# Splitting the output matmuls of a chunked mLSTM into two column halves of the TensorE array

## Chip, core and metric

The kernel runs on one core of a Trainium2 chip. The metric is the device time of one execution in microseconds; before the change the median of 3 runs is 906.31 us (905.92 to 907.33). Lower is better.

## What is computed

Three stages follow each other: an mLSTM recurrence over 768 tokens (4 batches, 8 heads, 40 values a head), then two gated feed-forward layers over the 3072 tokens.

```
for t in range(S):                                   # S = 768, per batch and head
    m_new  = max(f[t] + m, i[t])
    f_stab = exp(f[t] + m - m_new);  i_stab = exp(i[t] - m_new);  m = m_new
    C = f_stab * C + i_stab * outer(v[t], k[t])      # 40 x 40
    n = f_stab * n + i_stab * k[t]
    y[t] = sigmoid(o[t]) * (C @ q[t]) / max(|n @ q[t]|, 1)
x = y as [3072, 320]
x = (sigmoid(x @ w_gate) * (x @ w_val)) @ w_out      # 320 -> 1536 -> 320
h = x @ w_in                                         # 320 -> 2048 -> 320
out = (h * clip(h + 3, 0, 6) / 6) @ w_out2
```

## The kernel before

The recurrence is worked in 6 chunks of 128 tokens (`NC`, `L`), for 4 batches each, so there are 24 (chunk, batch) blocks. A chunk's tokens see each other through a 128 x 128 matrix per head, and the earlier chunks through a state `cst`. A block has three pieces:

- `att0`: eight matmuls for the products of keys and queries (line 303; 40 rows, alternately in the row halves from partition 0 and 64), then the decay matrix `dec` by scans and products on VectorE (lines 320 and 333), and the values with a gate factor, `vi`.
- `att1`, which the change touches: from chunk 1 on, four matmuls give what the state adds to the output (line 346, weights = 128 tokens of queries, streamed = a head pair's state, 82 columns, into `o_ps`); eight matmuls give what the chunk's own tokens add (line 356, weights = 128 columns of `dec`, streamed = `vi`, 41 columns, into `i_ps`). VectorE or ScalarE then reads both banks into `y` (lines 369, 372 and 374), divides (lines 376 to 381) and multiplies with the output gate into `yo` (line 383).
- `att2`: three transposes of `yo` (line 398), eight matmuls for the new state (line 405, 40 columns of weights, output alternately on partitions 0 and 64 of one bank), and the split of the transposed output into a rounded part and a rest (lines 415 and 416).

All these matmuls are in fp32. The feed-forward layers run in fp32r with each operand as a rounded part plus a rest: lines 439 to 446 for the way up, 480 and 490 for the way down of the first layer, 635 to 637 for that of the second. Their weights come packed as integers; `to_f32` unpacks them on VectorE (lines 108, 112 and 116, output `bits`), and half of them go back to memory first (line 515).

TensorE works in program order. Between the pieces of the blocks stand steps of the first layer: in the loop over `steps` each step takes one piece of a block, then one `m1_h` (16 matmuls) and one `m1_out` (8 matmuls). The tile scheduler may move rows, and does so in the first two chunks; from the third on a block's line 346 and line 356 stand together, with 24 large matmuls before and after. The second layer begins after the last block. The attention tiles `qk`, `vko` and `dec` have two buffers each; loads wait on SyncE's queue until a buffer is free, in one order with the weight loads and stores (lines 88, 91, 189, 190, 193, 515).

Of the kernel before, what the change touches and what calls it, by code (L numbers as in the profile page):

```python
# [18 lines left out]
B, H, S, D = 4, 8, 768, 40  # L19
# [3 lines left out]
NP = H // 2  # L23
D1 = D + 1
# [8 lines left out]
def mlstm_then_two_gated_ffn(  # L33
# [11 lines left out]
    nc = tc.nc  # L45
# [32 lines left out]
    cst = const.tile([P, B, NP, 2 * D1], F32, name="cst")  # L78
# [155 lines left out]
    def later_chunks():  # L234
# [40 lines left out]
        out=sel, in_=ident[:BH, :BH].rearrange("p (n two) -> p n two", two=2),  # L275
# [4 lines left out]
        out=odd[:, :, 0], in_=ident[:BH, :BH].rearrange("p (n two) -> p two n", two=2),  # L280
# [4 lines left out]
        out=par.rearrange("p (two n) -> p two n", two=2), in_=odd.to_broadcast([BH, 2, 64])  # L285
    )

    def scale_heads(out, in_, by, apart):

        if apart:  # L290
            for h in range(H):
                nc.scalar.mul(out=out[:, h, :], in_=in_[:, h, :], mul=by[:, h, :])
        else:
            nc.vector.tensor_tensor(out=out, in0=in_, in1=by.to_broadcast(list(out.shape)), op=ALU.mult)
# [45 lines left out]
    def att1(c, b, ps):  # L340
        a = at[c, b]
        dec, vi = a["dec"], a["vi"]
        if c > 0:
            o_ps = ps()
            for n in range(NP):
                nc.tensor.matmul(  # L346
                    out=o_ps[:, n * 2 * D1 : (n + 1) * 2 * D1],
                    lhsT=a["qk"][:, 0, n, :],
                    rhs=cst[:, b, n, :],
                    start=n == 0,  # L350
                    stop=n == NP - 1,
                    skip_group_check=True,
                )
        i_ps = ps()
        for h in range(H):
            nc.tensor.matmul(  # L356
                out=i_ps[:, h * D1 : (h + 1) * D1],
                lhsT=dec[:, h, :],
                rhs=vi[:, h, :],
                start=h == 0,  # L360
                stop=h == H - 1,
                skip_group_check=True,
            )
        i_v = i_ps[:, : H * D1].rearrange("p (h d) -> p h d", d=D1)
        y = ap.tile([P, H, D1], F32, tag="y", name="y")
        den = ap.tile([P, H, 1], F32, tag="den", name="den")
        if c > 0:
            o_v = o_ps[:, : H * D1].rearrange("p (h d) -> p h d", d=D1)
            nc.vector.tensor_tensor(
                out=y, in0=o_v, in1=gT[:, c, b].to_broadcast([P, H, D1]), op=ALU.mult  # L370
            )
            nc.vector.tensor_tensor(out=y, in0=y, in1=i_v, op=ALU.add)
        else:
            nc.scalar.copy(out=y, in_=i_v)
        nq = y[:, :, D:D1]
        nc.vector.scalar_tensor_tensor(
            out=den, in0=nq, scalar=-1.0, in1=nq, op0=ALU.mult, op1=ALU.max
        )
        nc.vector.tensor_scalar(out=den, in0=den, scalar1=1.0, scalar2=None, op0=ALU.max)
        nc.vector.reciprocal(out=den, in_=den)  # L380
        scale_heads(y[:, :, 0:D], y[:, :, 0:D], den, c == 1 or c == 0 and b < 2)
        yo = ap.tile([P, 3 * P], F32, tag="yo", name="yo")
        nc.vector.tensor_tensor(
            out=yo[:, :DM].rearrange("p (h d) -> p h d", d=D),
            in0=y[:, :, 0:D],
            in1=a["vko"][:, 2, :].rearrange("p (h d) -> p h d", d=D),
            op=ALU.mult,
        )

        nc.scalar.copy(out=yo[:, DM:], in_=yo[:, 2 * P : DM])  # L390
        a["yo"] = yo
# [162 lines left out]
    for b in range(2):  # L554
        work(1 + b, n_w1)
        for att in (att0, att1, att2):
            att(0, b, any_ps)
# [5 lines left out]
    halves = 4  # L563
# [11 lines left out]
    for i, (c, f, ts) in enumerate(steps):  # L575
# [4 lines left out]
        for _ in range(2 if i < 2 else 1):  # L580
            if pieces:
                cp, b, piece = pieces.pop(0)
                if cp > 0 and b == 0 and piece == 0:
                    x_tiles((1, cp))
                (att0, att1, att2)[piece](cp, b, ps_att)
                nxt = divmod(cp * B + b + 2, B)
                if cp > 0 and piece == 2 and nxt[0] < NC:
                    att_load(*nxt)
                    dec_load(*nxt)
# [141 lines left out]
```

## Time and profile before

| | us |
|---|---|
| median of 3 runs | 906.31 |
| the profiled execution, its own time | 904.88 |
| its span, first to last instruction | 903.0 |
| TensorE matmul busy | 873.6 (97%), 5077 instructions |
| TensorE weight loads busy | 752.1 (83%) |
| VectorE busy | 535.0 (59%) |
| ScalarE busy | 362.2 (40%) |
| 16 DMA engines, queue q1, mean share | 27.4% |

Busy time adds up what an engine spent in instructions; matmuls overlap each other, so the distance between the starts of two matmuls tells their pace, and the busy time of one does not. In the views, PE is TensorE, PEld its weight loads, DVE VectorE, ACT ScalarE, SP SyncE. A row of the timeline gives the start, the busy time of a merged run, the line, the output and its inputs, the shapes and the count. Column pairs such as 128*64 are active rows and columns of the array. TensorE's granted clock reads 1.00 in all stages.

### The profile page before, as it was taken

What the parts mean: (1) busy time and instruction counts of PE and PEld (TensorE: products, weight loads), DVE (VectorE), ACT (ScalarE), POOL (GpSimd) and SP (SyncE); (2) the same over time, 40 slices, a digit from 0 to 9 for tenths busy, and PEclk for the clock granted to TensorE, in tenths of its full rate; (3) what the DMA queues carried; (4) which work ended last, traced back from release to release, by engine and by line L of the source; (5) the groups of instructions that cost most, each with busy time, mean ns of one, the idle gap of its engine ahead of it and who ended that gap; (6) DMA issues with size and microseconds to landing.
All of it is one profiled execution on the core that took longest, in us unless ns stands there. A gap on an engine that the chain in (4) does not pass through costs nothing.

```text
span 903.0 us, 12844 instructions
## 1 busy us (share of the span) xinstructions
PE 873.6 (97%) x5077; PEld 752.1 (83%) x5077; DVE 535.0 (59%) x947; ACT 362.2 (40%) x720; POOL 2.5 (0%) x8
## 2 busy tenths in 40 slices
PE   2799999999999999999999999999999999999998
PEld 2688878887788888888888888999999999999997
DVE  7889999988765655555444555435344353443433
ACT  5675664333322232223223545334343343343432
POOL 1000000000000000000000000000000000000000
PEclk9999999999999999999999999999999999999999
DMA  9535545877422222223300431101001010000000
GB/s 327 226 133 183 201 162 168 290 258 250 156 75 70 84 90 69 69 91 104 104 1 1 131 98 67 36 1 65 1 30 36 1 65 1 3 28 1 30 1 30
DMA packets 25195, 84.22 MB, mean 93 GB/s; under 512 B 2608, under 2 KB 5872, under 8 KB 25136
## 3 DMA queue, kind: packets, MB, share of 16 engines
q1 hardware_dynamic: 25088, 83.31, 27.4%
q8 instruction: 40, 0.66, 0.3%
q14 instruction: 19, 0.16, 0.1%
q10 hardware_dynamic: 48, 0.10, 0.0%
HBM read 69.40 MB, written 13.99 MB: 92 GB/s over the span
## 4 chain that ended last, share of the span: by engine, by line
PE 90%; DVE 5%; DMA 2%; ACT 1%; issue 1%; SPq 0%; DVEq 0%; ACTq 0%
PE mm L443 12%; PE mm L445 12%; PE mm L444 12%; PE acc L480 10%; PE mm L439 7%; PE mm L446 6%; PE acc L637 5%; PE acc L636 5%; PE acc L635 5%; PE att L356 4%; PE acc L490 3%; PE att L303 2%; PE att L346 2%; PE att L637 2%; PE att L636 2%; PE att L635 2%
## 5 line engine op out<-in xcount | busy, mean ns | idle before, releaser
L443 PE MATMUL mm<-xh,w 128*128 128x512 f32 (+1 forms) x496 | 191.8, 387 | 0.0
L445 PE MATMUL mm<-xh,w 128*128 128x512 f32 (+1 forms) x496 | 191.0, 385 | 0.0
L444 PE MATMUL mm<-xl,w 128*128 128x512 f32 (+1 forms) x496 | 190.7, 385 | 0.0
L453 DVE TENSOR_TENSOR gl<-g,gh 128x512 fp32r<-128x512 f32 (+1 forms) x172 | 116.3, 676 | 99.3 <-ACT gh L452 98.8
L452 ACT CAST gh<-g 128x512 fp32r<-128x512 f32 (+1 forms) x172 | 104.9, 610 | 158.0 <-PE att L636 90.3
L617 DVE SCALAR_TENSOR_TENSOR g<-g,mm 128x512 f32<-128x512 f32 x96 | 66.0, 688 | 112.0 <-ACT g L616 112.0
L616 ACT ACTIVATE g<-mm,half 128x512 f32<-128x512 f32 x96 | 66.2, 690 | 112.1 <-PE mm L446 112.0
L445 PEld LDWEIGHTS mm<-xh,w 128*128 128x128 f32 x496 | 93.6, 189 | 19.2
L444 PEld LDWEIGHTS mm<-xl,w 128*128 128x128 f32 x496 | 93.8, 189 | 19.1
L443 PEld LDWEIGHTS mm<-xh,w 128*128 128x128 f32 x496 | 93.9, 189 | 15.0
L480 PE MATMUL acc<-gh,w 128*128 128x512 f32 (+1 forms) x304 | 102.5, 380 | 0.9 <-ACT w L150 0.5
L439 PE MATMUL mm<-xl,w 128*128 128x512 f32 (+1 forms) x248 | 101.0, 407 | 0.4 <-ACT g L465 0.4
L466 DVE TENSOR_TENSOR g<-g,mm 128x512 f32<-128x512 f32 (+1 forms) x76 | 50.0, 658 | 76.9 <-PE mm L446 75.7
L446 PE MATMUL mm<-xh,w 128*128 128x512 f32 (+1 forms) x248 | 95.3, 384 | 0.0
L465 ACT ACTIVATE g<-mm 128x512 f32<-128x512 f32 (+1 forms) x76 | 43.6, 574 | 116.6 <-PE mm L446 115.2
L637 PE MATMUL acc<-w,gl 128*128 128x320 f32 x288 | 89.0, 309 | 0.0
L636 PE MATMUL acc<-w,gh 128*128 128x320 f32 x288 | 88.9, 309 | 0.0
L635 PE MATMUL acc<-w,gh 128*128 128x320 f32 x288 | 88.8, 308 | 0.0
L480 PEld LDWEIGHTS acc<-gh,w 128*128 128x128 f32 x304 | 56.5, 188 | 13.0 <-ACT gh L452 1.6
L480 PE MATMUL acc<-gl,w 128*128 128x512 f32 (+1 forms) x152 | 57.8, 381 | 0.6 <-DVE gl L453 0.6
L635 PEld LDWEIGHTS acc<-w,gh 128*128 128x128 f32 x288 | 54.1, 188 | 1.8
L636 PEld LDWEIGHTS acc<-w,gh 128*128 128x128 f32 x288 | 54.1, 188 | 1.8
(145 smaller groups left out, 1154.3 us busy)
## 6 DMA issues: line engine op xcount, KB each, us to landing
raw<-in_w SPq DMA_DIRECT2D x20, 640.0 KB, 5.0
qk<-in_qkT SPq DMA_DIRECT2D x22, 512.0 KB, 3.7
dec<-fz_dram SPq DMA_DIRECT2D x22, 512.0 KB, 5.0
vko<-in_vko SPq DMA_DIRECT2D x22, 480.0 KB, 3.6
raw<-in_wo SPq DMA_DIRECT2D x14, 640.0 KB, 4.4
w_dram<-bits SPq DMA_DIRECT2D x16, 320.0 KB, 4.3
raw<-w_dram SPq DMA_DIRECT2D x16, 320.0 KB, 3.0
x_dram<-x SPq DMA_DIRECT2D x6, 768.0 KB, 5.9
```

The costliest lines, as they stand in the source:

```text
L439: nc.tensor.matmul(out=banks[j], lhsT=tail, rhs=xl[:, 2, :], start=True, stop=False)
L443: nc.tensor.matmul(out=banks[j], lhsT=hi, rhs=xh[:, k, :], start=False, stop=False)
L444: nc.tensor.matmul(out=banks[j], lhsT=hi, rhs=xl[:, k, :], start=False, stop=False)
L445: nc.tensor.matmul(out=banks[j], lhsT=lo, rhs=xh[:, k, :], start=False, stop=False)
L446: nc.tensor.matmul(out=banks[j], lhsT=tail, rhs=xh[:, 2, :], start=False, stop=True)
L452: nc.scalar.copy(out=gh, in_=g)
L453: nc.vector.tensor_tensor(out=gl, in0=g, in1=gh.bitcast(F32), op=ALU.subtract)
L480: nc.tensor.matmul(out=a[m], lhsT=lhsT, rhs=rhs, start=st and lhsT is hi and rhs is gh, stop=en and lhsT is lo, skip_group_check=True,)
L616: nc.scalar.activation(out=g[j], in_=banks[j], func=AF.Relu, scale=1.0 / 6.0, bias=half)
L635: nc.tensor.matmul(out=a, lhsT=gh[:, ts], rhs=hi, start=st, stop=False)
L636: nc.tensor.matmul(out=a, lhsT=gh[:, ts], rhs=lo, start=False, stop=False)
L637: nc.tensor.matmul(out=a, lhsT=gl[:, ts], rhs=hi, start=False, stop=en)
```

## The change

Each matmul of lines 346 and 356 becomes two, one for tokens 0 to 63 with its output on partitions 0 to 63, and one for tokens 64 to 127 on partitions 64 to 127. The streamed operand is the same for both. Weights per matmul fall from 128 columns to 64, and the number of matmuls doubles. In the changed file these are lines 349 and 360, and later lines move down by four.

```diff
     def att1(c, b, ps):
         a = at[c, b]
         dec, vi = a["dec"], a["vi"]
+
+        halves = (slice(0, 64), slice(64, 128))
         if c > 0:
             o_ps = ps()
             for n in range(NP):
+                for tt in halves:
+                    nc.tensor.matmul(
+                        out=o_ps[tt, n * 2 * D1 : (n + 1) * 2 * D1],
+                        lhsT=a["qk"][:, 0, n, tt],
+                        rhs=cst[:, b, n, :],
+                        start=n == 0,
+                        stop=n == NP - 1,
+                        skip_group_check=True,
+                    )
+        i_ps = ps()
+        for h in range(H):
+            for tt in halves:
                 nc.tensor.matmul(
-                    out=o_ps[:, n * 2 * D1 : (n + 1) * 2 * D1],
-                    lhsT=a["qk"][:, 0, n, :],
-                    rhs=cst[:, b, n, :],
-                    start=n == 0,
-                    stop=n == NP - 1,
+                    out=i_ps[tt, h * D1 : (h + 1) * D1],
+                    lhsT=dec[:, h, tt],
+                    rhs=vi[:, h, :],
+                    start=h == 0,
+                    stop=h == H - 1,
                     skip_group_check=True,
                 )
-        i_ps = ps()
-        for h in range(H):
-            nc.tensor.matmul(
-                out=i_ps[:, h * D1 : (h + 1) * D1],
-                lhsT=dec[:, h, :],
-                rhs=vi[:, h, :],
-                start=h == 0,
-                stop=h == H - 1,
-                skip_group_check=True,
-            )
```

TensorE's order in a block of the later chunks, before, from the last matmuls of a step to the first of the next (each row: line, operation, output and inputs, columns of weights x columns streamed, count):

```order
L480 MATMUL acc<-gh,w 128x512
L490 MATMUL acc<-gl,w 64x512
L490 MATMUL acc<-gh,w 128x512
L346 MATMUL att<-cst,qk 128x82 x4
L356 MATMUL att<-vi,dec 128x41 x8
L439 MATMUL mm<-xl,w 128x512
L443 MATMUL mm<-xh,w 128x512
```

and with the change:

```order
L484 MATMUL acc<-gh,w 128x512
L494 MATMUL acc<-gl,w 64x512
L494 MATMUL acc<-gh,w 128x512
L349 MATMUL att<-cst,qk 64x82 x8
L360 MATMUL att<-vi,dec 64x41 x16
L443 MATMUL mm<-xl,w 128x512
L447 MATMUL mm<-xh,w 128x512
```

The place of the block stays; twelve matmuls have become 24.

TensorE at the start of the program, the blocks of batches 0 to 2 in chunk 0, before:

```order
L303 MATMUL att<-qk 128x128 x7
L356 MATMUL acc<-vi,dec 128x41 x8
L356 MATMUL mm<-vi,dec 128x41
L303 MATMUL att<-early 128x128 x3
L356 MATMUL mm<-vi,dec 128x41 x7
L303 MATMUL att<-early 128x128 x5
```

and with the change:

```order
L303 MATMUL att<-qk 128x128 x7
L360 MATMUL acc<-vi,dec 64x41 x16
L360 MATMUL mm<-vi,dec 64x41 x2
L303 MATMUL att<-early 128x128 x3
L360 MATMUL mm<-vi,dec 64x41 x14
L303 MATMUL att<-early 128x128 x5
```

Here too nothing moves but the count.

SyncE's queue in chunk 2, the difference (`w_dram<-bits` is a store of unpacked weights, `raw` a load of packed ones):

```order
+L519 DMA w_dram<-bits 128x640
 L190 DMA vko<-in_vko 128x960
-L515 DMA w_dram<-bits 128x640
 L88 DMA raw<-in_wo 128x640
-L515 DMA w_dram<-bits 128x640
+L519 DMA w_dram<-bits 128x640
 L189 DMA qk<-in_qkT 128x1024
 L193 DMA dec<-fz_dram 128x1024
```

One load of `vko` now stands behind a store that stood behind it.

## Rows read from the trace of the kernel before

**Rows 1.** The page, chain that ended last, share of the span by engine.
```profile
PE 90%; DVE 5%; DMA 2%; ACT 1%; issue 1%; SPq 0%; DVEq 0%; ACTq 0%
```
**Rows 2.** Table by stage: stretch, length, busy time of each engine (instructions), PEclk, DMA share, GB/s.
```profile
0.00:60.00 60.00, 39.00 (x265) 35.48 (x266) 47.37 (x99) 41.83 (x120) 2.49 (x8) 1.00 0.67 247
60.00:150.00 90.00, 87.54 (x598) 72.33 (x597) 86.73 (x174) 52.86 (x143) 0.00 (x0) 1.00 0.52 167
150.00:240.00 90.00, 87.55 (x533) 71.70 (x532) 81.36 (x148) 31.80 (x59) 0.00 (x0) 1.00 0.71 239
240.00:480.00 240.00, 240.00 (x1435) 198.43 (x1434) 135.58 (x255) 61.90 (x123) 0.00 (x0) 1.00 0.24 78
```
**Rows 3.** The same table for line 356 alone: matmul busy, load busy (passes).
```profile
0.00:60.00 60.00, 13.41 (x64) 12.64 (x64) 1.00 0.67 247
60.00:150.00 90.00, 7.53 (x64) 7.62 (x64) 1.00 0.52 167
150.00:240.00 90.00, 7.66 (x64) 7.47 (x64) 1.00 0.71 239
240.00:480.00 240.00, 22.98 (x192) 22.40 (x192) 1.00 0.24 78
```
**Rows 4.** Groups by line and shape: count, busy us, mean ns, idle before.
```profile
L346 PE MATMUL att<-cst,qk 128*128 128x82 f32 x160 | 20.3, 270 | 0.0
```
**Rows 5.** Timeline of the weight loads, a late block: start, busy us, engine, line.
```profile
473.76 1.08 PEld L346 LDWEIGHTS att<-cst,qk 128*128 128x128 f32 x8
474.77 1.87 PEld L356 LDWEIGHTS att<-vi,dec 128*128 128x128 f32 x16
476.56 0.19 PEld L439 LDWEIGHTS mm<-xl,w 128*128 128x128 f32 x1
```
**Rows 6.** Timeline of the matmuls, the same block.
```profile
473.76 0.39 PE L490 MATMUL acc<-gh,w 128*128 128x512 f32 x1
473.99 1.01 PE L346 MATMUL att<-cst,qk 128*128 128x82 f32 x8
```
**Rows 7.** Timeline of the weight loads, a block of line 405.
```profile
384.22 0.39 PEld L405 LDWEIGHTS att<-vd,vko 128*40 128x40 f32 x16 [0.17 <-issue]
384.66 0.19 PEld L439 LDWEIGHTS mm<-xl,w 128*128 128x128 f32 x1
```
**Rows 8.** Groups of weight loads with 40, 64 and 128 columns.
```profile
L405 PEld LDWEIGHTS att<-vd,vko 128*40 128x40 f32 x256 | 6.2, 118 | 3.2 <-issue 1.7 <-PE att L398 1.1 <-DVE bits L108 0.2
L490 PEld LDWEIGHTS acc<-gl,w 128*64 128x64 f32 x76 | 10.2, 134 | 2.7
L490 PEld LDWEIGHTS acc<-gh,w 128*128 128x128 f32 x76 | 14.3, 188 | 5.9
```
**Rows 9.** Timeline of the weight loads, a block of line 303.
```profile
440.65 0.97 PEld L303 LDWEIGHTS att<-qk 40*128 40x128 f32 x16 [0.36 <-issue]
```
**Rows 10.** Timeline of the matmuls, the last one ahead of that block.
```profile
440.33 0.39 PE L490 MATMUL acc<-gh,w 128*128 128x512 f32 x1
```
**Rows 11.** Waits from 150 to 240 us: engine, line, releaser: us, times, longest.
```profile
PE att L398 <- DVE yo L383: 2.5, 1, 2.5
...
DVE vi L294 <- DMA vko<-in_vko: 1.6, 2, 1.4
```
**Rows 12.** The chain in order of time, 20 to 50 us: start, us, what.
```profile
20.93 3.77 PE acc L356 x16
...
40.89 2.29 PE att L356 x10
```
**Rows 13.** Timeline of VectorE at the start, with the idle time before a row.
```profile
25.19 0.17 DVE L376 SCALAR_TENSOR_TENSOR den<-y 128x8 f32<-128x8 f32 x1 [2.04 <-ACT y L374]
...
44.89 0.56 DVE L416 TENSOR_TENSOR xl<-mm,xh 128x384 fp32r<-128x384 f32 x1 [1.52 <-ACT xh L415]
```

## The prediction

> **What bounds the kernel now.** The chain of waits comes first: TensorE holds 90% of it [rows 1], so a microsecond taken from TensorE can show in the time. The table by stage then says where. From 240 to 480 us TensorE is busy for 240.00 of 240 us, while VectorE has 135.58 and the DMA engines a share of 0.24: nothing else is near its limit. From 60 to 150 us VectorE is busy for 86.73 of 90 us, so there two engines bind together; from 150 to 240 us VectorE has 81.36 of 90 and the DMAs 0.71; before 60 us TensorE has only 39.00 of 60 [rows 2]. The same table for line 356 alone counts its passes: 64, 64, 64 and 192 in these four stages, 384 in all, and nothing after 480 us [rows 3]; line 346 has 160 [rows 4]. The program has 24 x 8 = 192 matmuls on line 356 and 20 x 4 = 80 on line 346, so each fp32 matmul is two passes here, each with a weight load of its own.
>
> What sets the pace of such a pass? In a late block the loads of line 356 run from 474.77 to 476.56 us, 16 of them: 1.79/16 = 0.112 us each. Those of line 346 take (474.77 - 473.76 - 0.23)/7 = 0.111 us after the first [rows 5, 6]. Line 346 streams 82 columns and line 356 41, and the pace is one: the load of 128 columns sets it, not the stream.
>
> **What two column halves run at.** The trace already holds such a block. Line 405 writes its output alternately to partitions 0 and 64, so its 40-column loads go by turns to the two column halves, all 128 rows each. Its 16 loads begin within 0.39 - 0.12 = 0.27 us (the last lasts 0.118 us), seven steps from pair to pair: 0.039 us for two passes [rows 7, 8]. Could they be loads in series? A load takes 188 ns with 128 columns, 134 with 64 and 118 with 40 [rows 8], some 0.8 ns a column; two 40-column loads in series would need at least 0.064 us. So the halves load at the same time, and a pair costs one half's pace. The Trainium skill, "TensorE: Matmul & The Clock Gate", section "Part 3: Packing small matmuls — row/col tiling", says that weight loads overlap with running matmuls only where the row group differs. Two column halves share their row groups, so by that rule a new pair would take two loads in series and this change would only add cost; the row of line 405 speaks against it.
>
> Line 303 alternates in the row halves, with 128 columns loaded and 128 streamed: (0.97 - 0.19)/7 = 0.111 us a pair [rows 9]. Between the two rows I interpolate, 0.039 us at 40 columns and 0.111 at 128. A new line-356 pair loads 64 columns a half: 0.039 + 24 x 0.00082 = 0.058 us, against 0.112 for the one pass that it replaces. A new line-346 pair loads 64 but streams 82. No row tells which of the two binds; if the load, 0.058; if the stream, 0.039 + 41 x 0.00083 = 0.073; and at worst 0.111, no gain. I take 0.073, since line 303, which streams most, lies on the same slope.
>
> **The change part by part.** It adds 192 + 80 program matmuls, each of the new ones with half the columns, so 384 and 160 passes become 768 and 320. Operands, PSUM banks and the readers on VectorE stay; in chunk 1 and the start of chunk 2 the scheduler puts some rows elsewhere, in the late blocks none.
> - Line 356 in one (chunk, batch) block: 16 x (0.112 - 0.058) = 0.86 us less.
> - Line 346: 8 x (0.111 - 0.073) = 0.30 us less; bounds 8 x 0.053 = 0.42 and 0.
> - Going over to halves: after the last matmul of line 490 the first matmul comes 0.23 us later in the block of line 346, but 440.65 - 440.33 = 0.32 us in that of line 303 [rows 6, 9, 10]: 0.09 us. The first load is no longer hidden, an estimate of 0.05 us. Going back: line 405's last load begins at 384.22 + 0.27 = 384.49 us, the next matmul's at 384.66, 0.17 us against 0.112: 0.06 us [rows 7]. In all 0.20 us for each visit, with ends of 0.10 (line 303's step alone) and 0.35 (should the first pair also cost a second full load).
> - Block with both lines together: 0.86 + 0.30 - 0.20 = 0.96 us; ends 0.86 + 0 - 0.35 = 0.5 and 0.86 + 0.42 - 0.10 = 1.2.
>
> By stage, since cover differs:
> - 240 to 480 us: 192/16 = 12 blocks, TensorE alone binds: 12 x 0.96 = **11.5 us**, all on the path. VectorE's share rises by 5% of 135.58, far from its limit; no wait takes over.
> - 150 to 240 us: four blocks, 3.8 us. But TensorE stands still for 2.5 us at line 398, waiting for yo, and VectorE waits 1.6 us for vko in this stage [rows 11]; a faster TensorE meets that wait earlier. The scheduler also puts one vko load behind a store here. I take **2.5 us** (ends 0 and 3.8).
> - 60 to 150 us: four blocks, three of them with lines 346 and 356 apart, so two visits each: 0.96 + 3 x (1.16 - 0.40) = 3.2 us. VectorE has 90 - 86.73 = 3.3 us of idle time in the stage, and part of it is waiting for DMAs. I take **1.5 us** (ends 0 and 3.2).
> - 0 to 60 us: passes take twice as long here, 3.77/16 = 0.24 us [rows 12]. Two of these stand on the chain: 16 passes at 20.93 us and 10 at 40.89. With pairs at 2 x 0.058 = 0.116 us and visits at 0.40, they fall from 3.77 to 2.26 and from 2.29 to 1.56 us. I take **2.0 us** of these 2.2 (ends 0 and 3); VectorE waits 2.04 us for the copy of the first one's output and 1.52 us for what follows the second [rows 13], so the work behind moves up with them.
> - After 480 us: nothing is touched.
>
> Sum: 11.5 + 2.5 + 1.5 + 2.0 = 17.5 us. The profiled execution took 904.88 us (span 903.0), which becomes 887.4; the median of the runs, 906.31, is 1.4 us above it, so I predict **888.8 us**.
>
> **The rivals.**
> - *Only the late blocks pay.* Up to 240 us VectorE and the DMAs set the pace, and what TensorE saves is waited away: 906.3 - 11.5 = 894.8 us. For it: 86.73 of 90 us of VectorE. Against: the startup waits of VectorE for line 356's results. 27%.
> - *All of it carries*: 11.5 + 3.8 + 3.2 + 3 = 21.5, so 884.8 us. For it: TensorE's 90% of the chain. 12%.
> - *The halves don't overlap* (slower). Place: each pair of lines 346 and 356 in all 44 line blocks. A pair then costs two loads in series, 2 x 0.058 = 0.116 us against 0.112, so 544 x 0.004 = 2.2 us, and some 29 visits at 0.20 add 5.8: 914.3 us. It decides as soon as a pair takes over 0.104 us, where 24 x 0.008 us no longer pay for a visit. For it: both halves now stream the same operand and use all rows, and the order within a matmul's two passes is not mine to set. Against: line 405 also uses all rows and alternates in the same way. 7%. It is also the case in which the change does not do what it says. By the skill's rule above the time would be this one.
> - *Instructions arrive too slowly.* A block now has 48 passes in a row, and no fast run in the trace is longer than 16. If line 356's 32 passes came at the 0.112 us of any longer stretch, a block would lose 16 x 0.112 = 1.79 us, less 0.30, with a visit of 0.20: 1.7 us worse, 17 times: about 935 us. Against: line 405 shows no slowing in 16 passes. 3%. The Trainium skill, same page, section "Wait — 56ns, not 53.3ns?", gives about 62 ns for each matmul where the sequencer decodes in software; by that figure a block's 48 passes would take, as an estimate, 3.0 us where 24 x 0.112 = 2.7 stood, slower too. Line 405's passes, 0.02 us each, disagree, over 16 of them.
> - *Gain and visits cancel*, a pair near 0.104 us: 906. 3%.
>
> **How the numbers follow.** My forecast (885.5 to 891) has 48%. A difference under 0.2%, 1.8 us, can't be told from no change. Faster: 48 + 27 + 12 = 87%; same 3%; slower 7 + 3 = 10%. The range takes in the forecast and both faster rivals: its low end is all carried with visits at 0.10 us, 906.3 - 21.5 - 17 x 0.10 - 3 x 0.20 = 882; its high end the late blocks alone at 0.8 us each, 906.3 - 9.6 = 897.
>
> **What would show it.** In the late blocks: line 356's passes begin in pairs, and 16 pairs take about 0.93 us where 16 passes took 1.79; line 346's about 0.6 instead of 0.9; the next matmul of line 439 comes about 1 us sooner after line 490. In the table by stage the 240 us of dense TensorE become about 228. Wrong are the steps if a pair takes over 0.1 us (halves in series), if only line 346's pace stays (its stream), or if TensorE shows new waits before 240 us equal to what its blocks lost. Visits of half a microsecond would make the gain 8 us and the forecast wrong.

## The result and the profile after

The changed kernel takes 892.26 us (median of 4 runs, 891.48 to 894.13) against 906.82 for the kernel before (4 runs): a ratio of 0.9839, 95% interval 0.9814 to 0.9863. That is 14.6 us less where 17.5 were forecast. The profiled execution went from 904.88 to 892.28 us, 12.6 less. One run of the version with quarters and spread jobs, further below, took 1398.70 us at a mean granted clock of 0.568, and its median is that of the other three runs.

Busy time on the page of the changed kernel:

```profile
PE 856.3 (96%) x5621; PEld 724.4 (81%) x5621; DVE 534.9 (60%) x947; ACT 361.3 (41%) x720; POOL 2.5 (0%) x8
```

TensorE has 544 passes more (5621 against 5077) and is busy for 17 us less. The table by stage, to be held against [rows 2]; the last stretch is 10 us shorter, as the blocks end earlier:

```profile
0.00:60.00 60.00, 36.95 (x363) 31.88 (x364) 51.06 (x105) 44.42 (x129) 2.49 (x8) 1.00 0.70 258
60.00:150.00 90.00, 87.18 (x720) 69.32 (x719) 87.39 (x176) 52.37 (x138) 0.00 (x0) 1.00 0.51 168
150.00:240.00 90.00, 85.40 (x619) 66.65 (x618) 78.26 (x144) 31.64 (x59) 0.00 (x0) 0.96 0.68 231
240.00:470.00 230.00, 230.00 (x1685) 184.60 (x1686) 135.70 (x254) 59.72 (x120) 0.00 (x0) 1.00 0.24 82
```

From 240 us on TensorE is as dense as before. In the stretch before it, TensorE is busy for 85.40 us instead of 87.55 and the granted clock reads 0.96 instead of 1.00. Something went wrong there.

A late block on the timeline of the changed kernel's matmuls (line 494 was 490, 349 was 346, 360 was 356, 443 and 447 were 439 and 443):

```profile
461.92 0.39 PE L494 MATMUL acc<-gh,w 128*128 128x512 f32 x1
462.24 0.79 PE L349 MATMUL att<-cst,qk 128*64 128x82 f32 x16
462.86 1.08 PE L360 MATMUL att<-vi,dec 128*64 128x41 f32 x32
463.87 0.50 PE L443 MATMUL mm<-xl,w 128*128 128x512 f32 x1
464.21 0.39 PE L447 MATMUL mm<-xh,w 128*128 128x512 f32 x1
```

and the end of the same block before, which began as in [rows 6]:

```profile
476.58 0.48 PE L439 MATMUL mm<-xl,w 128*128 128x512 f32 x1
476.90 0.39 PE L443 MATMUL mm<-xh,w 128*128 128x512 f32 x1
```

From the last matmul of the step before to the second one of the next: 464.21 - 461.92 = 2.29 us, where it was 476.90 - 473.76 = 3.14. A late block saves **0.85 us**.

Where the rest went shows in when a block of the state's line begins:

| first row of the state's matmuls | before, us | after, us | gained so far |
|---|---|---|---|
| chunk 1, first block | 69.41 | 65.48 | 3.93 |
| chunk 2, first block | 152.12 | 147.40 | 4.72 |
| chunk 2, last block | 216.41 | 210.51 | 5.90 |
| chunk 3, first block | 240.46 | 238.23 | 2.23 |
| second matmul behind the last block | 476.90 | 464.21 | 12.69 |

Between 211 and 238 us 3.7 us were lost again. The timeline there, changed kernel:

```profile
218.70 0.39 PE L494 MATMUL acc<-gh,w 128*128 128x512 f32 x1
222.18 1.00 PE L402 MATMUL att<-ident,yo 128*128 128x128 f32 x3 [3.09 <-DVE yo L387]
223.81 0.79 PE L443 MATMUL mm<-xl,w 128*128 128x512 f32 x1
224.41 0.63 PE L447 MATMUL mm<-xh,w 128*128 128x512 f32 x1
224.83 0.63 PE L448 MATMUL mm<-xl,w 128*128 128x512 f32 x1
...
228.15 0.39 PE L448 MATMUL mm<-xl,w 128*128 128x512 f32 x1
```

and before, from the same place to the same matmul:

```profile
224.33 0.39 PE L490 MATMUL acc<-gh,w 128*128 128x512 f32 x1
227.17 0.52 PE L398 MATMUL att<-ident,yo 128*128 128x128 f32 x3 [2.45 <-DVE yo L383]
...
230.47 0.39 PE L444 MATMUL mm<-xl,w 128*128 128x512 f32 x1
```

Two things are to be seen. The stop at the transposes of `yo` grew from 2.84 us (224.33 to 227.17) to 3.48 (218.70 to 222.18). And after it the matmuls come 0.43 us apart instead of 0.23: from the transposes to the same matmul it takes 228.15 - 222.18 = 5.97 us instead of 230.47 - 227.17 = 3.30, so **2.7 us** went there. The table of the changed kernel for 220 to 230 us names the cause in its PEclk column:

```profile
220.00:225.00 5.00, 2.82 (x22) 2.09 (x23) 5.00 (x8) 1.96 (x4) 0.00 (x0) 0.62 0.47 151
225.00:230.00 5.00, 5.00 (x18) 3.97 (x17) 3.86 (x8) 0.96 (x2) 0.00 (x0) 0.70 0.48 142
```

A reading of 0.5 is the lower level, 1.2 GHz, so the two stretches hold 5 x 0.38/0.5 + 5 x 0.30/0.5 = 6.8 us at that level; in the execution of the kernel before, the clock stayed at 1.00 in both. All four runs of the changed kernel read a mean of 0.996 or 0.997, so the fall is not special to the profiled one. The stop's growth (0.64 us) and the slow stretch (2.7) make up 3.3 of the 3.7 us lost; most of the rest went in two short waits of line 484 just ahead of the stop.

### The profile page after: what moved, and what is told of

Its sections match the earlier page's. It is cut to its first block, busy times and chain, and to the rows that moved or that the text cites. A ratio compares the mean times of both kernels' runs of the same rounds, so it can differ in the third digit from the quotient of the medians.

```text
span 890.3 us, 13931 instructions
## 1 busy us (share of the span) xinstructions
PE 856.3 (96%) x5621; PEld 724.4 (81%) x5621; DVE 534.9 (60%) x947; ACT 361.3 (41%) x720; POOL 2.5 (0%) x8
## 4 chain that ended last, share of the span: by engine, by line
PE 75%; DVE 1%; issue 0%
PE mm L447 10%; PE mm L449 10%; PE mm L448 10%; PE acc L484 8%; PE mm L443 6%; PE mm L450 5%; PE acc L641 5%; PE acc L640 5%; PE acc L639 5%; PE acc L494 3%; PE att L641 2%; PE att L639 2%; PE att L640 2%; PE att L303 1%; PE att L360 1%; PE att L349 1%
```

## The experiments

Each ratio is against runs of the kernel before in the same group: 906.54 us for the first four versions, 907.43 for the next four and 906.68 for the last. In each view the line numbers are those of that version.

**Own tokens alone.** Line 360 in halves, the state's matmuls whole, as before.

```diff
-                for tt in halves:
-                    nc.tensor.matmul(out=o_ps[tt, ...], lhsT=a["qk"][:, 0, n, tt], ...)
+                nc.tensor.matmul(out=o_ps[:, ...], lhsT=a["qk"][:, 0, n, :], ...)
```

> Only the matmuls on the chunk's own tokens (line 356 before) are halved; those on the state stay whole. Theory: in a late block 16 pairs at 0.058 us replace 16 passes at 0.112 (0.85 us less) and one visit to the halves costs 0.33 us, so from line 490's last matmul to the second one of the next step 3.14 us becomes 2.62, 12 times 0.52 = 6.2 us from 240 us on, and some 898 us if nothing is lost before. Rival (a visit costs 0.20 us or less): 2.49 us a block, 7.9 us late. Rival (the stop of TensorE near 220 us is due to TensorE being ahead of VectorE): the start of the first block of chunk 3 gains less than the block of chunk 2 before it.

Measured: 891.17 us, ratio 0.984 (0.9808 to 0.9872). The matmul timeline, with the stop at the transposes, the first block of chunk 3 and a late block:

```profile
217.80 0.39 PE L493 MATMUL acc<-gh,w 128*128 128x512 f32 x1
219.57 0.52 PE L401 MATMUL att<-ident,yo 128*128 128x128 f32 x3 [1.37 <-DVE yo L386]
...
232.81 0.46 PE L348 MATMUL att<-cst,qk 128*128 128x82 f32 x3
...
459.64 0.39 PE L493 MATMUL acc<-gh,w 128*128 128x512 f32 x1
459.87 1.01 PE L348 MATMUL att<-cst,qk 128*128 128x82 f32 x8
460.81 1.13 PE L359 MATMUL att<-vi,dec 128*64 128x41 f32 x32
...
462.21 0.40 PE L446 MATMUL mm<-xh,w 128*128 128x512 f32 x1
```

462.21 - 459.64 = 2.57 us, 0.57 less than before, between the theory's 2.62 and the rival's 2.49 and nearer to the theory. The time was missed by 7 us: before 240 us this version gains 7.7 us (first block of chunk 3 at 232.81 instead of 240.46), because its stop at the transposes is 1.77 us long (217.80 to 219.57) and its granted clock stays at 1.00. The third guess, that TensorE's lead alone makes the stop, falls: this version is as early as the changed kernel there and stops for half as long. With a smaller gain in each block it is as fast as the changed kernel (890.41 to 894.92 us against 891.48 to 894.13), so there the stop and the clock took back what the state's halves brought.

**The state alone.** Line 349 in halves, the own tokens' matmuls whole.

```diff
-            for tt in halves:
-                nc.tensor.matmul(out=i_ps[tt, ...], lhsT=dec[:, h, tt], ...)
+            nc.tensor.matmul(out=i_ps[:, ...], lhsT=dec[:, h, :], ...)
```

> Only the matmuls on the state (line 346 before) are halved. Theory: 8 pairs at 0.070 us replace 8 passes at 0.112 (0.33 us less) and the visit takes 0.33 us, so the late blocks stay at 3.14 us and the time within 2 us of before, 905 to 909. Rival (a visit costs 0.20 us or less): 0.13 us or more less a block, at least 1.6 us from 240 us on. Rival (the two lines' gains add up without visits): 4 us from 240 us on, 903 us.

Measured: 905.57 us, ratio 0.9995 (0.9981 to 1.001): no difference, as the theory had it. The block:

```profile
473.52 0.39 PE L493 MATMUL acc<-gh,w 128*128 128x512 f32 x1
473.84 0.79 PE L349 MATMUL att<-cst,qk 128*64 128x82 f32 x16
474.56 1.98 PE L359 MATMUL att<-vi,dec 128*128 128x41 f32 x16
...
476.69 0.39 PE L446 MATMUL mm<-xh,w 128*128 128x512 f32 x1
```

476.69 - 473.52 = 3.17 us, 0.03 more than before. The two together price a visit to the halves, if it costs the same with either line: each version pays one, the changed kernel pays one for both, so the visit is what is missing in the sum, 0.85 - (0.57 - 0.03) = **0.31 us**. Without it the own tokens bring 0.88 us a block and the state 0.28.

**The halves one after the other.** All matmuls in halves, but each line first for the lower half over all heads, then for the upper.

```diff
-            for n in range(NP):
-                for tt in halves:
+            for tt in halves:
+                for n in range(NP):
...
-        for h in range(H):
-            for tt in halves:
+        for tt in halves:
+            for h in range(H):
```

> The changed kernel's matmuls, all of them, but each line first for tokens 0 to 63 over all heads, then for tokens 64 to 127: neighbours sit in the same column half. Theory (the gain comes from neighbours in different halves loading at the same time): 16 passes at 0.071 us and 32 at 0.058 stand in series, the block takes 1.1 + 1.9 + 0.8 = 3.8 us against 3.14 before and 2.29 changed, so slower than before by 0.65 us in 16 blocks, about 917 us. Rival (64 columns a load are enough, order is of no matter): 2.29 us a block and 892 us.

Measured: 907.41 us, ratio 1.0008 (0.9989 to 1.0028). The block, with the rows at the seam between the two lines left out:

```profile
478.09 0.39 PE L494 MATMUL acc<-gh,w 128*128 128x512 f32 x1
478.41 0.91 PE L349 MATMUL att<-cst,qk 128*64 128x82 f32 x13
...
479.35 1.60 PE L360 MATMUL att<-vi,dec 128*64 128x41 f32 x28
...
481.22 0.39 PE L447 MATMUL mm<-xh,w 128*128 128x512 f32 x1
```

481.22 - 478.09 = 3.13 us: same instructions, same operands, and the whole gain of a block is gone. So it comes from neighbours that sit in different halves and run at the same time. In the changed kernel such neighbours also stream the same operand, which this order takes away as well; but line 405's pairs in the kernel before stream different operands and still run at 0.039 us a pair. The size was missed (3.8 us and some 917 us expected): where one half's run ends and the other's begins, the second starts while the first still works, and the rows left out show lines 349 and 360 by turns, from 479.10 to 479.31 us. Within a run passes of line 360 stand 0.058 us apart.

**The late chunks alone.** Halves from chunk 3 on.

```diff
-        halves = (slice(0, 64), slice(64, 128))
+        halves = (slice(0, 64), slice(64, 128)) if c > 2 else (slice(0, 128),)
```

> The halves are used in chunks 3 to 5 alone; chunks 0 to 2 stay as before. Theory (12 late blocks save 0.85 us each, all on the path; before 240 us the whole change nets some 2 us): 10.2 us less than before, 896.6 us, the stop of TensorE near 227 us stays at 2.8 us and its granted clock at 1.00 there. Rival (the early halves carry more than the profile of one execution shows): over 899 us. Rival (the early halves cost time in sum): under 892 us.

Measured: 897.25 us, ratio 0.9897 (0.9863 to 0.9931), so 9.3 us less, near the 10.2 expected, though the interval also takes in the first rival's 899 us. Not expected: the profiled execution, the slowest of the four, has a stop of 2.97 us near 229 us (227.26 to 230.23), and here the clock falls after it:

```profile
225.00:230.00 5.00, 2.65 (x12) 1.82 (x10) 4.90 (x13) 0.76 (x1) 0.00 (x0) 1.00 0.57 202
230.00:240.00 10.00, 9.77 (x61) 7.69 (x62) 9.33 (x16) 2.85 (x7) 0.00 (x0) 0.83 0.49 170
```

Its four runs fall apart accordingly: 894.71 and 895.54 us at a mean granted clock of 1.000, 898.96 and 899.21 at 0.997 and 0.998.

**Unpacking jobs spread, kernel before and changed kernel.** Each of the 16 jobs that unpack the second layer's weights is held on VectorE behind an instruction of its own step of the first layer.

```diff
-            work(f % 3 == 1, n_conv)
+            with tc.issue_after(last_gl[0]):
+                work(f % 3 == 1, n_conv)
```

(`last_gl` holds the latest VectorE instruction of line 453, the rest of `g`.)

> The kernel before, with the 16 unpacking jobs for the second layer's weights held back on VectorE to one for every three steps of chunks 1 to 4 (before, they are all done by 240 us). Theory (from 150 to 240 us VectorE's backlog of these jobs makes TensorE stop): the stop of 2.8 us near 227 us and the short ones after 140 us go, 903 to 904 us. Rival (TensorE waits there for the DMA of vko, not for VectorE): the stop stays, 906 to 907 us.

> The changed kernel with the same spreading of the unpacking jobs. Theory (what the early blocks save is waited away and a slower clock adds to it): the stops after 140 us (5 to 6 us together) and the stretch with a granted clock of 0.6 to 0.7 near 225 us (some 2.8 us) go, 883 to 886 us, and the distance to the kernel before with spread jobs is 17 to 20 us where it was 14.6. Rival (the backlog only moves later, or the wait is for a DMA): 890 to 893 us.

Measured: before with spread jobs 902.79 us, ratio to the kernel before 0.995 (0.9934 to 0.9967); changed with spread jobs 884.38 us, 0.9746 (0.9731 to 0.976). VectorE's time in unpacking (writes and reads of `bits`) from 150 to 240 us, first in the kernel before, then in the changed kernel with spread jobs:

```profile
150.00:240.00 90.00, 31.96 (x45) 0.00 (x0) 1.00 0.71 239
```
```profile
150.00:240.00 90.00, 8.48 (x12) 0.00 (x0) 1.00 0.42 143
```

And the stage in that last version, all engines, with the place of the stop:

```profile
150.00:240.00 90.00, 90.00 (x667) 72.03 (x666) 64.64 (x122) 26.66 (x53) 0.00 (x0) 1.00 0.42 143
```
```profile
216.97 0.39 PE L495 MATMUL acc<-gh,w 128*128 128x512 f32 x1
217.20 0.49 PE L402 MATMUL att<-ident,yo 128*128 128x128 f32 x3
```

TensorE is dense, the transposes follow 0.23 us after the matmul ahead of them, the clock is 1.00. The backlog of jobs makes the stop, as the theory had it. It can do so through VectorE's time or through the jobs' DMAs, whose share falls with them from 0.71 to 0.42. VectorE's rows tell part of this. In the changed kernel, between the block's matmuls and `yo`:

```profile
215.44 0.49 DVE L294 TENSOR_TENSOR vi<-vko,iT 128x320 f32<-128x320 f32 x1 [0.78 <-DMA vko<-in_vko]
...
220.82 0.82 DVE L116 SCALAR_TENSOR_TENSOR bits<-u,bits 128x640 int32<-128x640 int32 x1
221.55 0.48 DVE L387 TENSOR_TENSOR yo<-y,vko 128x320 f32<-128x320 f32 x1
```

and at the same place with spread jobs:

```profile
213.62 0.49 DVE L387 TENSOR_TENSOR yo<-y,vko 128x320 f32<-128x320 f32 x1
```

From the block's first matmul to `yo` it takes 221.55 - 210.51 = 11.0 us in the changed kernel and 213.62 - 209.98 = 3.6 with spread jobs. In the changed kernel five instructions on `bits`, 3.8 us of busy time, stand between the end of the block's matmuls at 212.2 us and `yo`; with spread jobs none does. VectorE also waited there for DMAs, 1.33 us (up to 211.86) for a store of unpacked weights and 0.78 us for `vko`. So by these rows VectorE's own time is the larger part; no run takes the DMAs away and leaves VectorE's work. The split is worth 902.79 - 884.38 = **18.4 us** where this stop is gone, against 14.6 with the jobs where they were.

**Quarters for the own tokens.** Four parts of 32 tokens for line 360, halves for the state; once with the jobs as they were, once spread.

```diff
+        quarters = [slice(32 * k, 32 * k + 32) for k in range(4)]
...
-            for tt in halves:
+            for tt in quarters:
                 nc.tensor.matmul(
                     out=i_ps[tt, h * D1 : (h + 1) * D1],
```

> The changed kernel with the own-token matmuls cut into four quarters of 32 tokens; those on the state stay in halves. Theory (the pace of a group is that of one part's load or stream, 32 columns loaded, 41 streamed: as line 405, 0.039 us): 16 groups take 0.62 us where 16 pairs take 0.93, 0.31 us less a block, less one more visit between halves and quarters of 0.1 to 0.3: the block falls from 2.29 to between 2.0 and 2.3 us, 0 to 3.7 us late. Rival (passes can't follow each other faster than line 405's 0.019 us): 64 passes take 1.2 us, the block grows to 2.5 to 2.9 us and the time by 3 to 8 us.

> Quarters for the own tokens and spread unpacking jobs together. Theory: the spread jobs' time less what the quarters bring in a block, without an interaction: 880 to 886 us. Rival (passes at 0.019 us at best): 886 to 893 us.

Measured: 889.60 us, ratio 0.9809 (0.979 to 0.9829), and 882.48 us (three runs, 881.64 to 883.75), 0.9727 (0.9711 to 0.9744). The block of the first:

```profile
458.67 0.39 PE L495 MATMUL acc<-gh,w 128*128 128x512 f32 x1
458.98 0.79 PE L350 MATMUL att<-cst,qk 128*64 128x82 f32 x16
459.71 0.82 PE L361 MATMUL att<-vi,dec 128*32 128x41 f32 x64
...
460.79 0.39 PE L448 MATMUL mm<-xh,w 128*128 128x512 f32 x1
```

460.79 - 458.67 = 2.12 us, 0.17 less than with halves, inside the theory's 2.0 to 2.3. The 64 passes start within 0.62 us (0.82 less the last one's 0.2), 0.010 us each: the rival pace of 0.019 us falls. With spread jobs the interval overlaps that of the halves, so between 884.4 and 882.5 the runs don't decide.

**Quarters for both lines, jobs spread.** The edit against the version before:

```diff
-                for tt in halves:
+                for tt in quarters:
                     nc.tensor.matmul(
                         out=o_ps[tt, n * 2 * D1 : (n + 1) * 2 * D1],
```

> Spread unpacking jobs, and both lines in quarters of 32 tokens, so that a block changes the way the array is divided only on entering and leaving. Theory (a group's pace is its longest part: for the state the stream of 82 columns, 0.070 us with halves and quarters alike; going from halves to quarters inside a block costs some 0.1 us): the late block falls from 2.13 to 2.03 us, 1 to 2 us less than with halves for the state, 881 to 883 us. Rival (the state's pace is set by its loads): groups at 0.039 us, a block of 1.8 us and 877 to 879 us. Rival (more parts, more passes, more to issue): a block over 2.13 us.

Measured: 880.46 us (5 runs, 880.24 to 881.32), ratio 0.9711 (0.9695 to 0.9728), half a microsecond below the 881 to 883 expected and above the first rival's 877 to 879. It is the lowest median, though its interval overlaps that of the version before. The block:

```profile
451.45 0.39 PE L495 MATMUL acc<-gh,w 128*128 128x512 f32 x1
451.77 0.78 PE L349 MATMUL att<-cst,qk 128*32 128x82 f32 x32
452.37 0.81 PE L360 MATMUL att<-vi,dec 128*32 128x41 f32 x64
...
453.44 0.39 PE L447 MATMUL mm<-xh,w 128*128 128x512 f32 x1
```

453.44 - 451.45 = 1.99 us, 0.13 less. The state's part keeps its length (0.60 us to the first row of line 360, against 0.62 with halves in the changed kernel), so its stream of 82 columns sets its pace and not its load; what is saved is the step from halves to quarters, which made that distance 0.73 us in the block above (458.98 to 459.71).

## Why the prediction was right, and where it was off

The direction, the range (882 to 897) and the mechanism in a block held; the middle was 3.5 us too low. The measured 892.26 lies outside the forecast's own band (885.5 to 891) and nearer to the rival in which only the late blocks pay (894.8) than to the forecast (888.8): in the profiled executions 10.5 of the 12.7 us come from the late blocks. The rival's reason was another, though. What was saved early was not waited away as it came: 5.9 us of it had arrived by 210 us, and 3.7 were lost again around one stop. That the sum came as near as it did is in part luck, since 1.9 us more than charged at the start covered part of the 5.0 missing from 150 to 240 us. Step by step:

- **The pace of a pair.** Predicted 0.058 us for the own tokens and 0.073 for the state. Shown: 0.058 apart within one half, and the state's groups at (462.86 - 462.24 - 0.12)/7 = 0.071 us after a first one of 0.12. The interpolation between lines 405 and 303 held, and with it the choice of the stream as the state's limit; the last experiment shows that choice directly.
- **Overlap of column halves.** The row of line 405 was read rightly and the slower rival fell: with the same instructions in another order the block takes 3.13 us. The Trainium skill's rule ("TensorE: Matmul & The Clock Gate", "Part 3: Packing small matmuls — row/col tiling"), by which loads overlap running matmuls only where row groups differ, doesn't hold here: pairs share all row groups and stand 0.058 us apart, not 0.116.
- **Issue.** 48 passes in a row did not slow down, nor did 64 quarter passes at 0.010 us. The Trainium skill's 62 ns a matmul ("TensorE: Matmul & The Clock Gate", "Wait — 56ns, not 53.3ns?") binds in none of these runs, as its own condition, decoding in software, allows.
- **The visit and the block.** 0.20 us was predicted, with 0.35 as the upper end; the two experiments with one line each give 0.31. So a block saves 0.85 us instead of 0.96, and the 12 late blocks 12.69 - 2.23 = 10.5 us instead of 11.5. Part of what is called the visit is an overcount of the old block: the 24 old passes were charged 0.112 us each, 2.69 in all, but from 473.99 [rows 6] to the next step's matmul at 476.58 they took 2.59, since the first interval of each line is shorter, 0.07 us.
- **0 to 60 us, too low.** 2.0 us predicted with an end of 3; 3.9 gained up to the first block of chunk 1. The gain is 1.5 us at the copy of the first output (ScalarE writes `y` at 23.25 us instead of 24.72) and 3.3 at the first large matmul (42.55 instead of 45.85): work behind both of VectorE's waits moved up, and more than the passes themselves saved. Another 0.75 comes from TensorE's pace, for which the prediction had no term. The first large matmuls, 256 columns each, stand 0.21 us apart and then 0.12, from 48.76 us on before and from 43.76 on with the change, so the first 16 take 3.26 us before and 2.51 after. That is close to the ratio of the two clock levels near 225 us (0.43 and 0.23 us for 512 columns), though the clock column reads 1.00 from 0 to 60 us in both tables, so here that column is not to be relied on. How much of the 3.9 is the change's own is not settled by one execution of each: two versions whose chunk 0 is that of the kernel before, state alone and late chunks alone, come to that block at 71.03 and 70.52 us, not 69.41.
- **60 to 150 us, near.** 4.72 - 3.93 = 0.8 us against 1.5: VectorE is busy for 87.39 of 90 us, as [rows 2] had warned.
- **150 to 240 us, the step that failed.** Predicted "2.5 us (ends 0 and 3.8)"; measured 2.23 - 4.72 = -2.5, outside both ends. "A faster TensorE meets that wait earlier" was right as far as it went: the stop grew by 0.6 us. The prediction had named new waits before 240 us as a sign against its steps, and for this stage the sign came. Two things had no term. A stop has a price beyond its length, since the clock fell after it: 2.7 us. And the lower end was set at zero, though nothing excluded a loss. With the unpacking jobs spread, stop and loss are gone and the split brings 18.4 us. That is close to the 17.5 of the forecast, but by other parts: between the two profiled executions with spread jobs 3.7 us are gained up to chunk 1, 0.4 up to chunk 2, 3.4 up to chunk 3 and 10.5 behind it, 18.0 in all, where the forecast had 2.0, 1.5, 2.5 and 11.5.

What is left open: why the stop is 1.8 us with the own tokens alone and 3.5 with both lines in halves, and why the clock fell in some executions and not in others. The order on VectorE and SyncE differs between all these versions, and no run here changes that order by itself.

## What to carry to other kernels

Where small matmuls are held up by their weight loads, cut the output into column parts and let neighbours alternate between the parts: a group then costs the longest load or stream of one part, and in one part after the other it brings nothing. Entering and leaving such a stretch cost 0.31 us here, so put matmuls of the kind together (8 state passes alone were not worth a visit). When one engine gets faster, look at the places where it already waits: price a stop as its length plus what the clock takes afterwards, and see whether work that another engine does early, without need, can be spread.

## What the runs showed of the hardware that was not expected

- The clock after a stop. From the start of the last matmul to that of the next, TensorE's stop is 3.48 us in the changed kernel, 3.49 with one half after the other and 2.97 with late halves, and the granted clock fell to its lower level around all three; with 2.84 us in the profiled execution of the kernel before and 2.87 with quarters for the own tokens it did not. Nor does it take a stop of this length: with quarters for both lines the clock fell near 80 us (0.68 from 80 to 85 us), where no stop was longer than 1.4. Runs of one kernel differ in this: of 19 runs of the kernel before, seven at a mean granted clock of 1.000 took 903.8 to 905.0 us, three at 0.996 or 0.997 took 907.8 to 909.6, and the nine between lie at 904.5 to 909.3. It is not the whole of the spread, since in the last group runs at 1.000 took 904.6 to 907.7. The profiled execution, at 904.88 us, a mean of 0.999 and 1.00 in every stage, lies with the undisturbed ones; that the clock explains the 1.4 us between it and the median, which the prediction only added, is likely by their size but not shown.
- Column parts work as lanes of their own: in the experiment with one half after the other, rows of lines 349 and 360 come by turns at the seam (479.10 to 479.31 us), which by the program's order are the upper half of the state's line and the lower half of the own tokens', with different operands.
- Four quarters take 0.010 us a pass, about half of line 405's 0.019.
